# Moving a gate behind a decoding operation, splitting two gated blocks early, and emptying an accumulator before the next gate

## The chip, the cores and the metric

The kernel runs on one core of a Trainium2 chip. Its engines are TensorE (PE in the rows; its weight loads are PEld), VectorE (DVE), ScalarE (ACT), GpSimd (POOL) and SyncE (SP), which issues nearly all loads. Each engine works through its own list of instructions in order and waits on semaphores for the others. The metric is the device time of one execution in microseconds (us).

## The reference, cut to what matters

Three layers follow each other: a windowed attention, a gated feed-forward layer, and a layer of 8 experts with a router. The change lies in the second:

```python
def _moe_ref(x, w_in, w_out):
    h = x @ w_in                        # 3072 x 512 by 512 x 2048
    relu6 = np.clip(h + 3.0, 0.0, 6.0)
    g = h * relu6 / 6.0                 # the gate
    return (g @ w_out).astype(np.float32)
```

The weights `w_in` and `w_out` come as 64-bit floats and are taken as pairs of 32-bit integers.

## The kernel before, in words

The 3072 tokens go through the feed-forward layer in blocks. Block 0 holds four tiles of 128 tokens (512 columns), block 1 two tiles, each later block three. The 2048 hidden features are cut into 16 groups of 128; a pass is the work on one group `f`. Each product is made exact enough by three matmuls, because every operand is kept as a rounded high half and the low rest: high by high, low by high and high by low.

Block 0 is special, since the weights are decoded while it runs.

**First stage** (`mm1(0, f)`, matmuls at L395). In pass `f` TensorE multiplies group `f + 1` (12 matmuls of 512 columns into one of two banks, `h0` and `h1`), then `dec(1, lambda: gate0(f, hp))` decodes one piece of weights and gates group `f`. `decode_w` takes piece `n` from a raw tile (three buffers) with three VectorE operations: the first (L369) writes `d`, the second (L372) adds bits to `d`, the third (L373) writes the float in `dec` (two buffers). Then `load_w(n + 3)` asks SyncE for the next raw tile, ScalarE rounds the piece to its high half (L378), and GpSimd subtracts for the low half (L379). In pass `f` piece `n = f + 3` is decoded, so from pass 13 on the pieces are those of `w_out` (n = 16 and above). The gate is an activation on ScalarE (L431) and a multiplication on VectorE (L433); it frees the bank that TensorE wants for group `f + 2`. The gated block is put somewhere until the second stage (`g_home`): for the last two groups that is a `dec` buffer. Attention steps of tiles 4 to 6 stand between the passes (`side`): `a` (transposes of queries and keys, copies into `kt`), `s` (scores, maximum, exponential), `n` (sums), `p` and `v` (probabilities times values, after which SyncE issues 16 small loads), `x` (result transposed and split).

**Second stage** (`mm2(0, f)`, matmuls at L451). The groups come in the order `STEP` = 14, 15, 0, 1, ... 13. For each, `split_g` rounds the gated block into its high half on ScalarE (L439) and subtracts for the low half (L440; GpSimd, for one group VectorE), and TensorE adds 12 matmuls of 512 columns into four accumulators: three banks `acc`, and the bank `h0`. Meanwhile pieces 18 to 31 are decoded with `d` in the bank `h1`.

**Block 1 and later.** `mm1(1, 0)` (12 matmuls of 256 columns into `h1`), its gate (L408, L409) and its split (L403, L404) are followed by `evac(0)`, which empties the four accumulators of block 0, two on VectorE (L468) and two on ScalarE (L470). `mm1(1, 1)` writes to `h0`, the fourth accumulator's bank.

Of the kernel before, what the change touches and what calls it, by code (L numbers as in the profile page):

```python
# [7 lines left out]
F32 = mybir.dt.float32  # L8
# [6 lines left out]
ALU = mybir.AluOpType  # L15
# [15 lines left out]
def attn_moe_kernel(ctx, tc, q, k, v, mem_k, mem_v, w_in, w_out, emb, tau, w1, w2, out, dbg=None):  # L31
# [322 lines left out]
    def decode_w(n, first=None):  # L354

        f = FORD[n]
        t = raw.pop(n)
        if n < KF:
            t = t.rearrange("p c n t -> p (c n) t")
            dst_h, dst_l = w_in_h[:, :, f * P:(f + 1) * P], w_in_l[:, :, f * P:(f + 1) * P]  # L360
        else:
            for hl in range(2):
                if (hl, f // 2) not in wo:
                    wo[hl, f // 2] = pair(hl, f // 2, F32R)
            dst_h, dst_l = (wo[hl, f // 2][:, f % 2, :] for hl in range(2))
        lo, hi = t[:, :, 0], t[:, :, 1]
        d = late["dw"]().bitcast(I32)
        w = sb.tile([P, 512], I32, tag="dec", name="dec", bufs=2)
        nc.vector.tensor_scalar(out=d, in0=hi, scalar1=0x07FFFFFF, scalar2=3, op0=ALU.bitwise_and, op1=ALU.logical_shift_left)  # L369
        if first:  # L370
            first()
        nc.vector.scalar_tensor_tensor(out=d, in0=lo, scalar=29, in1=d, op0=ALU.logical_shift_right, op1=ALU.bitwise_or)  # L372
        nc.vector.scalar_tensor_tensor(out=w, in0=hi, scalar=-0x40000000, in1=d, op0=ALU.bitwise_and, op1=ALU.bitwise_or)  # L373
        load_w(n + 3)
        wf = w.bitcast(F32)
        if n < KF:
            wf = wf.rearrange("p (c n) -> p c n", c=KD)
        nc.scalar.copy(out=dst_h, in_=wf)  # L378
        nc.gpsimd.tensor_tensor(out=dst_l, in0=wf, in1=dst_h.bitcast(F32), op=ALU.subtract)  # L379
# [33 lines left out]
    def g_home(f):  # L413

        n_ = BS[0] * P
        if f >= KF - 2:
            return [(sb.tile([P, n_], F32, tag="dec", name="g0", bufs=2), 0, n_)]
        if f >= KF - 4:
            if f == KF - 4:
                keep["r"] = sb.tile([P, BT], F32, tag="g", name="g0r", bufs=1)  # L420
            w = "gh" if f == KF - 4 else "gl"
            o = (f % 2) * P
            return [(sb.tile([P, BT], F32, tag=w, name="g0", bufs=2), 0, BT), (keep["r"][:, o:o + P], BT, n_)]
        if f % 2 == 0:
            keep["p"] = pair(1, f // 2 + 1, F32)
        return [(keep["p"][:, f % 2, :], 0, n_)]

    def gate0(f, hp):
        keep[f] = g_home(f)
        for g, a, z in keep[f]:  # L430
            nc.scalar.activation(out=g, in_=hp[:, a:z], func=AF.Relu, bias=three)  # L431
        for g, a, z in keep[f]:
            nc.vector.scalar_tensor_tensor(out=g, in0=g, scalar=6.0, in1=hp[:, a:z], op0=ALU.min, op1=ALU.mult)  # L433

    def split_g(t, eng=None):
        f = STEP[t]
        gh, gl = (xT[0][i][1][:, 1 + t % 2, :] for i in range(2))
        for g, a, z in keep.pop(f):
            nc.scalar.copy(out=gh[:, a:z], in_=g)  # L439
            (eng or nc.gpsimd).tensor_tensor(out=gl[:, a:z], in0=g, in1=gh[:, a:z].bitcast(F32), op=ALU.subtract)  # L440
        g_t[0, f] = (gh, gl)
# [301 lines left out]
    def T_x(n, px=None):  # L743
        xg = xg_t.pop(n)
        gate = small([P, 1], name="m_gate", bufs=4)
        V.tensor_copy(out=gate, in_=xg[:, DM:DM + 1])
        m_t[n] = (gate, m_t[n])
        px = bank("att", 1) if px is None else px
        for j in range(KD):
            nc.tensor.transpose(px[:, j * P:(j + 1) * P], xg[:, j * P:(j + 1) * P], ident)  # L750
        th = sb.tile([P, KD + KE, P], F32R, tag="xh", name="th", bufs=2)
        tl = sb.tile([P, KD + KE, P], F32R, tag="xl", name="tl", bufs=2)
        x3 = px.rearrange("p (j s) -> p j s", j=KD)
        nc.scalar.copy(out=th[:, 0:KD, :], in_=x3)  # L754
        V.tensor_tensor(out=tl[:, 0:KD, :], in0=x3, in1=th[:, 0:KD, :].bitcast(F32), op=ALU.subtract)  # L755
        xt_t[n] = (th, tl)
# [168 lines left out]
    with tc.manual_schedule():  # L925
# [119 lines left out]
        for f in range(KF):  # L1045
            nxt = mm1(0, f + 1) if f + 1 < KF else None
            if f < KF - 1:
                dec(1, lambda: gate0(f, hp))
            else:
                gate0(f, hp)  # L1050
            if f in side:
                side[f]()
            hp = nxt
        a4[5]()
        split_g(0)
        split_g(1, nc.vector)
        pdw2 = bank("h", 2)
        late["dw"] = lambda: pdw2
        side = {0: a5[0], 2: a5[1], 3: a5[2], 4: a5[3], 6: a5[4], 8: a5[5], 9: a6[0], 10: a6[1], 12: a6[2], 13: a6[3], 15: a6[4]}
        for t in range(KF):  # L1060
            mm2(0, STEP[t], first=STEP[0], last=STEP[-1])
            if t + 2 < KF:
# [12 lines left out]
        for bl in range(NB):  # L1075
            slot, pre_ = {}, {}
            if bl == 0:
                continue
            if bl + 1 < NB:
                if bl == 1:  # L1080
                    slot[0] = [a6[5]]
                for a in range(bl == 1, TB):
                    st = stages(F0[bl + 1] + a)
                    for o, f_ in zip((0, 2, 3, 4, 6, 7) if bl == 1 else (0, 1, 2, 3, 4, 5), st):
                        slot.setdefault((1, 8)[a - 1] + o if bl == 1 else 5 * a + o, []).insert(0, f_)
            if bl:
                d = 2 if bl == 1 else 0
                for t in range(BS[bl - 1]):
                    (wt, f), (wl, f2) = (RT4 if bl == 1 else RT)[t], (RL4 if bl == 1 else RL)[t]
                    (pre_, slot)[wt].setdefault(f, []).append(lambda t=t: r_t(bl - 1, t, spare(bl)))  # L1090
                    (pre_, slot)[wl].setdefault(f2, []).insert(0, lambda t=t: r_l(bl - 1, t))
                    slot.setdefault((8, 8, 9, 9)[t] + d // 2, []).append(lambda t=t: r_ss(bl - 1, t))
                slot.setdefault(8 + d, []).append(lambda: r_route(bl - 1))
                slot.setdefault(9 + d, []).append(lambda: r_rank(bl - 1))
                slot.setdefault(10 + d, []).append(lambda: r_sel(bl - 1))
                slot.setdefault(11 + d, []).append(lambda: r_list(bl - 1))
                slot.setdefault(12 + d, []).append(lambda: r_exp(bl - 1))
                slot.setdefault(12 + d, []).append(lambda: r_gate(bl - 1))
                if bl == EB + 1:
                    slot.setdefault(12, []).append(pick_first)  # L1100
                    slot.setdefault(14, []).append(pick_rest)
            if bl == NB - 1:
                at_ctx.close()
                p2["pool"] = ctx.enter_context(tc.tile_pool(name="p2", bufs=1, side="right", reuse_waits="tile"))
                for n in range(NE):
                    load_x(("E", n))
                eE = [nc.values_load(e0i[0:1, n:n + 1], engines=[SP], min_val=0, max_val=E - 1) for n in range(2)]
                todo = [(st, p, i) for p in range(4) for st in range(2) for i in range(2)]
                rws = {}

                def pre(n=1):
                    for _ in range(n):
                        if todo:
                            st, p, i = todo.pop(0)
                            rws[st, p, i] = load_half(p, i, eE[st])

                def go(st, p, i, eng=None):
                    split_half(st, p, i, rws.pop((st, p, i)), eng)
                    pre()

                pre(RW)
                for n, f in enumerate(SP_):
                    slot.setdefault(f, []).append(lambda n=n: go(n // 2 % 2, n // 4, n % 2, nc.gpsimd if n in PG else None))
                slot.setdefault(1, []).append(plan_const)
                slot.setdefault(13, []).append(lambda: T_x(("E", 0)))
            mm1(bl, 0)
            if bl:
                evac(bl - 1)
            for f in range(KF):
                for g_ in pre_.get(f, []):  # L1130
                    g_()
                if f + 1 < KF:
                    mm1(bl, f + 1)
                for g_ in slot.get(f, []):
                    g_()
                if bl < NB - 1 or f < KF - 1:
                    mm2(bl, f)
# [147 lines left out]
```

## Time and profile before

| | us |
|---|---|
| median of 3 runs | 1066.66 |
| lowest and highest run | 1066.11, 1069.86 |
| the profiled execution | 1062.98 |
| its span | 1061.2 |

The span is what the profile shows from first to last instruction; the profiled execution took 1.8 us more. Its mean granted TensorE clock is 0.985 of full speed.

### The profile page before, as it was taken

How to read it: one execution, taken by the hardware profiler on the slowest of the kernel's cores; microseconds unless marked ns; L12 is line 12 of the kernel's file. 1: busy time of each engine (PE TensorE's matmuls, PEld its weight loads, DVE VectorE, ACT ScalarE, POOL GpSimd, SP SyncE). 2: the span in 40 equal slices, each digit the busy share in tenths (PEclk: the TensorE clock that was granted, in tenths of full speed). 3: DMA queues.
4: the chain of work that ended last, by engine and by line, in shares of the span. 5: the costliest groups of instructions: out<-in, count | busy, mean ns of one | idle time of the engine just before them, and what ended most of it. 6: DMA issues, size and time to landing. Idle time of an engine off the chain costs nothing.

```text
span 1061.2 us, 22705 instructions
## 1 busy us (share of the span) xinstructions
PE 1013.5 (96%) x8350; PEld 855.5 (81%) x8350; DVE 519.3 (49%) x1194; ACT 429.4 (40%) x769; POOL 153.4 (14%) x155
## 2 busy tenths in 40 slices
PE   8787998999999999999999999998999999999994
PEld 4565777878888888888888888886888888888883
DVE  5676774554544544544544454755124433326530
ACT  5343443434333433434424424562235434336531
POOL 1133670000000000000000000043112211112210
PEclk9899899999999999999999999998999999999998
DMA  9655441152121122122211023331134514347510
GB/s 193 147 157 173 144 140 39 39 71 44 40 60 39 39 61 45 30 61 48 46 52 38 11 70 107 125 98 64 38 111 152 167 52 134 103 138 245 207 50 22
DMA packets 133914, 95.50 MB, mean 90 GB/s; under 512 B 100789, under 2 KB 109013, under 8 KB 133792
## 3 DMA queue, kind: packets, MB, share of 16 engines
q1 hardware_dynamic: 129184, 80.51, 27.6%
q0 software_dynamic: 4448, 13.42, 3.9%
q8 instruction: 67, 1.10, 0.4%
q14 instruction: 55, 0.45, 0.1%
q10 hardware_dynamic: 160, 0.02, 0.0%
HBM read 156.83 MB, written 13.38 MB: 160 GB/s over the span
## 4 chain that ended last, share of the span: by engine, by line
PE 78%; DVE 7%; issue 5%; ACT 3%; DMA 2%; POOL 1%; SPq 1%; POOLq 0%; DVEq 0%; ACTq 0%
PE acc L451 22%; PE h L395 20%; PE acc L799 12%; PE h L768 12%; PE s L777 2%; PE s L182 2%; PE s L294 1%; PE s L236 1%; DVE dec L373 1%; PE att L750 1%; PE att L280 1%; PE att L182 1%; DMA out_dram<-r,m_tid 1%; DMA raw_in<-in_moe_w_in_dram 1%; PE att L488 1%
## 5 line engine op out<-in xcount | busy, mean ns | idle before, releaser
L451 PE MATMUL acc<-wo,gh 128*128 128x512 f32 x640 | 206.5, 404 | 0.5 <-DVE x L468 0.3
L395 PE MATMUL h<-xh,w_in_h 128*128 128x384 f32 (+2 forms) x512 | 176.2, 344 | 10.6 <-DVE wo L433 4.0
L395 PE MATMUL h<-xl,w_in_h 128*128 128x384 f32 (+2 forms) x512 | 173.1, 338 | 0.1
L395 PE MATMUL h<-xh,w_in_l 128*128 128x384 f32 (+2 forms) x512 | 172.6, 337 | 0.0
L408 ACT ACTIVATE g<-h,three 128x384 f32<-128x384 f32 (+1 forms) x112 | 63.4, 566 | 173.9 <-PE h L395 172.1
L409 DVE SCALAR_TENSOR_TENSOR g<-g,h 128x384 f32<-128x384 f32 (+1 forms) x112 | 59.7, 533 | 143.5 <-ACT g L408 143.4
L451 PEld LDWEIGHTS acc<-wo,gh 128*128 128x128 f32 x640 | 113.1, 188 | 20.0 <-DVE x L468 0.7
L451 PE MATMUL acc<-wo,gl 128*128 128x512 f32 x320 | 126.1, 394 | 0.0
L395 PEld LDWEIGHTS h<-xh,w_in_h 128*128 128x128 f32 x512 | 96.5, 188 | 21.1 <-DVE wo L433 6.9
L395 PEld LDWEIGHTS h<-xl,w_in_h 128*128 128x128 f32 x512 | 96.6, 189 | 7.1 <-DVE xl L331 1.0
L395 PEld LDWEIGHTS h<-xh,w_in_l 128*128 128x128 f32 x512 | 96.4, 188 | 2.9
L404 DVE TENSOR_TENSOR gl<-g,gh 128x384 fp32r<-128x384 f32 (+1 forms) x112 | 60.8, 543 | 63.2 <-ACT gh L403 63.2
L403 ACT CAST gh<-g 128x384 fp32r<-128x384 f32 (+1 forms) x112 | 55.8, 498 | 74.0 <-DVE g L409 74.0
L755 DVE TENSOR_TENSOR tl<-att,th 128x512 fp32r<-128x512 f32 x26 | 18.0, 691 | 114.7 <-ACT th L754 108.4
L538 POOL TENSOR_TENSOR rn_y<-ss,half 128x3 f32<-128x3 f32 (+2 forms) x8 | 6.9, 860 | 464.9 <-ACT junk L528 464.9
L451 PEld LDWEIGHTS acc<-wo,gl 128*128 128x128 f32 x320 | 60.1, 188 | 13.9 <-DVE gl L404 0.3
L736 POOL DMA_INDIRECT xg<-xb,m_ix x27 | 27.9, 1032 | 260.2 <-PE h L768 210.7
L799 PE MATMUL acc<-wo,th 128*128 128x512 f32 x192 | 60.6, 397 | 0.0
L754 ACT CAST th<-att 128x512 fp32r<-128x512 f32 x26 | 15.3, 587 | 106.6 <-PE acc L799 104.9
L771 ACT ACTIVATE hs<-h 128x512 f32<-128x512 f32 x54 | 32.1, 597 | 64.4 <-PE h L768 60.5
L799 PE MATMUL acc<-w_in_h,th 128*128 128x512 f32 x120 | 49.5, 412 | 0.0
L768 PE MATMUL h<-wo,th 128*128 128x512 f32 x192 | 48.9, 397 | 0.0
(311 smaller groups left out, 1845.9 us busy)
## 6 DMA issues: line engine op xcount, KB each, us to landing
rw<-in_moe_w_dram SPq DMA_DIRECT2D x136, 512.0 KB
vw<-in_v_dram SPq DMA_DIRECT2D x176, 56.0 KB
raw_in<-in_moe_w_in_dram SPq DMA_DIRECT2D x16, 512.0 KB
raw_out<-in_moe_w_out_dram SPq DMA_DIRECT2D x16, 512.0 KB
k_t<-in_k_dram SPq DMA_DIRECT2D x24, 256.0 KB
q_t<-in_q_dram SPq DMA_DIRECT2D x24, 256.0 KB
xb<-x SPq DMA_DIRECT2D x20, 256.5 KB
xb<-x SPq DMA_DIRECT2D x4, 256.0 KB
```

The costliest lines, as they stand in the source:

```text
L182: nc.tensor.transpose(dst[:, j * P:(j + 1) * P], t[:, 2 * j:2 * j + 2, :].rearrange("p a d -> p (a d)"), ident)
L395: nc.tensor.matmul(hp, lhsT=wt[:, c, f * P:(f + 1) * P], rhs=xc, start=(n == 0), stop=(n == 3 * KD - 1))
L403: nc.scalar.copy(out=gh, in_=g)
L404: nc.vector.tensor_tensor(out=gl, in0=g, in1=gh.bitcast(F32), op=ALU.subtract)
L408: nc.scalar.activation(out=g, in_=hp, func=AF.Relu, bias=three)
L409: nc.vector.scalar_tensor_tensor(out=g, in0=g, scalar=6.0, in1=hp, op0=ALU.min, op1=ALU.mult)
L451: nc.tensor.matmul(acc[bl][t], lhsT=gt[:, t * P:(t + 1) * P], rhs=wo[hl, f // 2][:, f % 2, :], start=(f == first and n == 0), stop=(f == l ...
L736: nc.gpsimd.indirect_dma_start(out=t[:, :], out_offset=None, in_=src, in_offset=bass.IndirectOffsetOnAxis(ap=ix[:, 0:1], axis=0), bounds_c ...
L768: nc.tensor.matmul(hp, lhsT=a[:, kk, :], rhs=wpart(st, hl, p, kk), start=(kk == 0 and a is th and hl == 0), stop=(kk == KD - 1 and a is tl))
L771: nc.scalar.activation(out=h_t[n][:, p, :], in_=hp_t.pop((n, p)), func=AF.Relu)
L777: nc.tensor.transpose(hp[:, j * P:(j + 1) * P], h[:, j * P:(j + 1) * P], ident)
L799: nc.tensor.matmul(o, lhsT=a[:, KD + f, :], rhs=wpart(st, hl, 2 + half, kk), start=(f == 0 and c == 0), stop=(f == KE - 1 and c == 2))
```

## The change

Three edits. In `decode_w` the gate (`first()`) now stands behind the second decoding operation and ahead of the third. The last two gated blocks of block 0 no longer go into `dec` buffers: 384 of their columns go into the second buffers of `gh` and `gl`, the other 128 into columns 256 to 383 of `g0r` (one place for both groups, used one after the other), and they are split on VectorE right behind their gate. The step `x` of tile 4 (`a4[5]`), which stood between the stages, now stands behind the second stage's first group, together with step `a` of tile 5. `evac(0)` now stands ahead of `mm1(1, 0)`.

```diff
@@ decode_w
         nc.vector.tensor_scalar(out=d, in0=hi, scalar1=0x07FFFFFF, scalar2=3, op0=ALU.bitwise_and, op1=ALU.logical_shift_left)
+        nc.vector.scalar_tensor_tensor(out=d, in0=lo, scalar=29, in1=d, op0=ALU.logical_shift_right, op1=ALU.bitwise_or)
         if first:
             first()
-        nc.vector.scalar_tensor_tensor(out=d, in0=lo, scalar=29, in1=d, op0=ALU.logical_shift_right, op1=ALU.bitwise_or)
         nc.vector.scalar_tensor_tensor(out=w, in0=hi, scalar=-0x40000000, in1=d, op0=ALU.bitwise_and, op1=ALU.bitwise_or)
@@ g_home
-        if f >= KF - 2:
-            return [(sb.tile([P, n_], F32, tag="dec", name="g0", bufs=2), 0, n_)]
         if f >= KF - 4:
             if f == KF - 4:
                 keep["r"] = sb.tile([P, BT], F32, tag="g", name="g0r", bufs=1)
-            w = "gh" if f == KF - 4 else "gl"
-            o = (f % 2) * P
+            w = "gh" if f % 2 == 0 else "gl"
+            o = min(f - KF + 4, 2) * P
@@ first stage and start of the second
                 gate0(f, hp)
+            if f in STEP[0:2]:
+                split_g(STEP.index(f), nc.vector)
             if f in side:
                 side[f]()
             hp = nxt
-        a4[5]()
-        split_g(0)
-        split_g(1, nc.vector)
         pdw2 = bank("h", 2)
         late["dw"] = lambda: pdw2
-        side = {0: a5[0], 2: a5[1], ...
+        x4, a50 = a4[5], a5[0]
+        side = {0: lambda: (x4(), a50()), 2: a5[1], ...
@@ blocks
+            if bl == 1:
+                evac(0)
             mm1(bl, 0)
-            if bl:
+            if bl > 1:
                 evac(bl - 1)
```

In the changed kernel the lines behind `g_home` have numbers that are 2 lower. On VectorE, in each of the first 15 passes of the first stage (here pass 0; `acc` is the bank that holds `d`, `wo` the home of the gated block):

```order
 L369 TENSOR_SCALAR acc<-raw_in 128x512
-L433 SCALAR_TENSOR_TENSOR wo_838<-wo_838,h_809 128x512
-L372 SCALAR_TENSOR_TENSOR acc<-raw_in,acc 128x512
+L370 SCALAR_TENSOR_TENSOR acc<-raw_in,acc 128x512
+L431 SCALAR_TENSOR_TENSOR wo_839<-wo_839,h_809 128x512
 L373 SCALAR_TENSOR_TENSOR dec<-raw_in,acc 128x512
```

The gate has changed places with the second decoding operation. On ScalarE, from the activation of group 14 on, before (`g_1314` and `g_1323` are groups 14 and 15):

```order
L431 ACTIVATE g_1314<-h_1269,three 128x512
L378 CAST wo_1282<-dec 128x512
L431 ACTIVATE g_1323<-h_1298,three 128x512
L329 CAST xh<-att 128x4x128
L439 CAST xh<-g_1314 128x512
L439 CAST xh<-g_1323 128x512
L439 CAST xh<-wo_838 128x512
L378 CAST wo_1358<-dec 128x512
```

And now (`g_1315` and `g_1329` with parts of `g0r`):

```order
L429 ACTIVATE g_1315<-h_1269,three 128x384
L429 ACTIVATE g0r<-h_1269,three 128x128
L378 CAST wo_1282<-dec 128x512
L437 CAST xh<-g_1315 128x384
L437 CAST xh<-g0r 128x128
L429 ACTIVATE g_1329<-h_1298,three 128x384
L429 ACTIVATE g0r<-h_1298,three 128x128
L437 CAST xh<-g_1329 128x384
L437 CAST xh<-g0r 128x128
L437 CAST xh<-wo_839 128x512
L378 CAST wo_1357<-dec 128x512
L329 CAST xh<-att 128x4x128
```

Group 14's two roundings stand ahead of group 15's activations, all four are in two parts, and the copy for step `x` of tile 4 (`xh<-att`) has moved behind the first rounding and the first decoding of the second stage. On VectorE at the start of block 1, before (`h_1930` is the product of `mm1(1, 0)`, `h_1343` the fourth accumulator):

```order
L301 TENSOR_TENSOR xo<-s_1887,sm 128x2x4x64
L409 SCALAR_TENSOR_TENSOR g<-g,h_1930 128x256
L404 TENSOR_TENSOR gl<-g,gh 128x256
L468 TENSOR_SCALAR x_1951<-h_1343 128x512
L468 TENSOR_SCALAR x_1950<-acc 128x512
```

And now:

```order
L301 TENSOR_TENSOR xo<-s_1895,sm 128x2x4x64
L466 TENSOR_SCALAR x_1939<-h_1342 128x512
L466 TENSOR_SCALAR x_1938<-acc 128x512
L409 SCALAR_TENSOR_TENSOR g<-g,h_1945 128x256
L404 TENSOR_TENSOR gl<-g,gh 128x256
```

Both accumulators of VectorE are emptied ahead of the gate and the split.

## Rows read from the trace of the kernel before

**Rows 1.** Page, part 1: busy time, share of the span, instructions

```profile
PE 1013.5 (96%) x8350; PEld 855.5 (81%) x8350; DVE 519.3 (49%) x1194; ACT 429.4 (40%) x769; POOL 153.4 (14%) x155
```

**Rows 2.** Stretches: length, busy time of each engine, clock, DMA share, GB/s

```profile
43.84:102.22 58.38, 52.19 (x332) 38.94 (x333) 40.60 (x70) 21.21 (x43) 18.59 (x15) 0.97 0.52 153
102.22:107.70 5.48, 0.60 (x6) 0.36 (x4) 2.63 (x5) 2.35 (x5) 1.66 (x2) 0.77 0.43 161
107.70:112.85 5.15, 5.01 (x13) 3.49 (x13) 3.61 (x5) 0.47 (x1) 1.28 (x1) 0.58 0.01 5
112.85:163.37 50.52, 49.18 (x465) 38.84 (x463) 34.27 (x60) 21.77 (x39) 36.82 (x33) 1.00 0.47 146
...
88.00:96.00 8.00, 6.02 (x25) 4.33 (x24) 5.22 (x10) 2.57 (x5) 2.58 (x2) 1.00 0.76 233
```

**Rows 3.** TensorE's waits, 40 to 170 us: total, times, longest

```profile
PE acc L451 <- ACT xh L439: 4.9, 1, 4.9
PE h L395 <- DVE wo L433: 4.0, 6, 1.6
PE h L395 <- DVE x L468: 2.6, 1, 2.6
PE h L395 <- DVE g0r L433: 2.2, 2, 1.7
```

**Rows 4.** Timeline of VectorE, one pass: start, length, [idle before, releaser]

```profile
86.92 0.69 DVE L433 SCALAR_TENSOR_TENSOR wo<-wo,h 128x512 f32<-128x512 f32 x1 [0.67 <-ACT wo L431]
87.52 0.69 DVE L372 SCALAR_TENSOR_TENSOR acc<-raw_in,acc 128x512 int32<-128x512 int32 x1
88.32 0.69 DVE L373 SCALAR_TENSOR_TENSOR dec<-raw_in,acc 128x512 int32<-128x512 int32 x1
...
90.28 0.69 DVE L433 SCALAR_TENSOR_TENSOR wo<-wo,h 128x512 f32<-128x512 f32 x1 [0.67 <-ACT wo L431]
```

**Rows 5.** Timeline of ScalarE in the same pass

```profile
89.04 0.62 ACT L378 CAST w_in_h<-dec 128x512 fp32r<-128x512 f32 x1 [2.15 <-DVE dec L373]
89.57 0.68 ACT L431 ACTIVATE wo<-h,three 128x512 f32<-128x512 f32 x1
```

**Rows 6.** Timeline of VectorE: gate of pass 2, behind the copies into kt

```profile
57.59 0.68 DVE L433 SCALAR_TENSOR_TENSOR wo<-wo,h 128x512 f32<-128x512 f32 x1
```

**Rows 7.** Chain that ended last, 79 to 96 us: start, length, what

```profile
82.31 4.11 DMA raw_in<-in_moe_w_in_dram
...
90.26 3.98 DMA raw_in<-in_moe_w_in_dram
```

**Rows 8.** Timeline of TensorE between the stages

```profile
99.33 0.47 PE L395 MATMUL h<-xh,w_in_h 128*128 128x512 f32 x1 [0.54 <-DVE g0r L433]
...
102.22 0.60 PE L182 MATMUL att<-ident,xo 128*128 128x128 f32 x4
107.70 1.22 PE L451 MATMUL acc<-wo,xh 128*128 128x512 f32 x2 [4.88 <-ACT xh L439]
```

**Rows 9.** Timeline of ScalarE: activation of group 15

```profile
105.97 0.69 ACT L431 ACTIVATE g<-h,three 128x512 f32<-128x512 f32 x1 [1.37 <-POOL wo L379]
```

**Rows 10.** Timeline of all engines: the low halves of groups 14 and 15

```profile
107.72 1.28 POOL L440 TENSOR_TENSOR xl<-g,xh 128x512 fp32r<-128x512 f32 x1 [1.79 <-ACT xh L439]
108.20 1.35 DVE L440 TENSOR_TENSOR xl<-g,xh 128x512 fp32r<-128x512 f32 x1 [0.22 <-ACT xh L439]
```

**Rows 11.** VectorE's groups by form: busy, mean ns, idle before

```profile
L404 DVE TENSOR_TENSOR gl<-g,gh 128x384 fp32r<-128x384 f32 x96 | 54.0, 563 | 55.7 <-ACT gh L403 55.7
```

**Rows 12.** Timeline of TensorE at the start of block 1

```profile
164.75 0.28 PE L395 MATMUL h<-xh,w_in_l 128*128 128x256 f32 x1
167.60 0.39 PE L395 MATMUL h<-xh,w_in_h 128*128 128x256 f32 x1 [2.58 <-DVE x L468]
```

**Rows 13.** Timeline of VectorE there

```profile
163.58 0.69 DVE L301 TENSOR_TENSOR xo<-s,sm 128x512 f32<-128x512 f32 x1 [6.35 <-PE s L294]
...
166.87 0.68 DVE L468 TENSOR_SCALAR x<-h 128x512 f32<-128x512 f32 x1
```

More of the change, by code (lines that the diff above doesn't have):

```diff
@@ L1053, in attn_moe_kernel @@
             hp = nxt
-        a4[5]()
-        split_g(0)
-        split_g(1, nc.vector)
         pdw2 = bank("h", 2)
         late["dw"] = lambda: pdw2
-        side = {0: a5[0], 2: a5[1], 3: a5[2], 4: a5[3], 6: a5[4], 8: a5[5], 9: a6[0], 10: a6[1], 12: a6[2], 13: a6[3], 15: a6[4]}
+        x4, a50 = a4[5], a5[0]
+        side = {0: lambda: (x4(), a50()), 2: a5[1], 3: a5[2], 4: a5[3], 6: a5[4], 8: a5[5], 9: a6[0], 10: a6[1], 12: a6[2], 13: a6[3], 15: a6[4]}
         for t in range(KF):
```

## The prediction, as it was put on record before the changed kernel ran

> **What bounds the kernel now.** I began with the page's busy shares: TensorE is busy 96% of the span [rows 1], so time can only be won where TensorE stands still or runs slowly. The stretches show where that is near the edits. In the first stage (43.84 to 102.22) it is busy 52.19 of 58.38 us. Between the stages (102.22 to 107.70) it does 0.60 us of work, and the 12 matmuls that follow take 5.15 us at a mean clock of 0.58. In the second stage (112.85 to 163.37) only 1.3 of 50.5 us are idle [rows 2]. The waits name the causes: 6.2 us in eight waits for the gate on VectorE (L433), 4.9 us in one wait for ScalarE's rounding between the stages (L439), 2.6 us in one wait for `evac` on VectorE (L468) [rows 3]. Each edit aims at one of these. The 13.7 us, and some 2.4 us of slow clock behind the long one, are all there is to win.
>
> **Edit 1, the gate behind the second operation.** One pass without attention work is a closed loop [rows 4, 5]: gate to second operation 0.60, to third 0.80, to ScalarE's rounding 0.72, to the next activation (behind the rounding in ScalarE's list) 0.53, to the next gate 0.71. The sum, 3.36, is the distance between two gates (86.92 to 90.28). VectorE stands idle for 0.67 us ahead of the gate, with the first operation already done. With the second operation there as well, the loop is 0.60 + 0.72 + 0.53 + 0.71 = 2.56. VectorE's own four operations need 0.60 three times and, the second now right behind the first, 0.60 to 0.80 once (I take 0.7): 2.5. TensorE's 12 matmuls need up to 2.9 (99.33 to 102.22 [rows 8]; a little less without a wait ahead of them). So TensorE becomes the slowest, and a pass can win about 0.5.
>
> Passes with attention work win less. I walked all 15 with these durations. In pass 2 the copies into `kt` already make VectorE the late one: its gate has no idle time ahead of it [rows 6]. Now two operations stand ahead of it, and it comes 0.35 later than before. The gates' gain over the old starts runs: pass 1 0.55, pass 2 -0.35, passes 3 and 4 0.45, pass 5 0.55 (sums on VectorE), then 1.35, 2.1 and 2.9 in passes 6 to 8. The third operation of pass 8, no longer behind the second, gains 3.7. From there loads rule. That operation releases the raw tile whose load begins at 82.31 and takes 4.11 us. The 16 small loads of step `v` hold SyncE until 90.26, when the next raw load goes out and takes 3.98 [rows 7]. These 11.9 us don't shrink, while passes 9 to 11 do: VectorE's wait for that tile grows from 1.9 to about 2.7 us (estimates of my walk), and the gate of pass 12 stands behind one more operation. The gain of 3.7 is kept, and no more is added: the last group's product begins at 95.65 in place of 99.33 [rows 8] and ends at 98.45. **Gain 3.7**; bounds 0 (attention work or loads hold every pass) and 6.2 (every wait of rows 3 for the gate).
>
> **Edit 2, the last two blocks.** Before: the activation of group 15 waited until GpSimd had read a `dec` buffer (1.37 of idle [rows 9]); ScalarE's roundings stood behind it and behind step `x`; TensorE waited 4.88 [rows 8] and then ran slowly [rows 2]. From the end of the last product to the end of group 14's matmuls: 112.85 - 102.22 = 10.63.
>
> After, in my walk: the third operation of pass 14 at 98.15, ScalarE's rounding of piece 17 0.72 later, then the 384 columns of group 14, done at 99.95. TensorE begins there, 1.5 us after its last product. Its third matmul needs the low half. That subtraction on VectorE has two inputs in SBUF, and GpSimd works on piece 17's low half from 99.55 to 100.85. Before, just this pair met: VectorE's took 1.35 us for 512 columns and ended 0.55 after GpSimd's (109.55 against 109.00) [rows 10], where 384 columns cost 0.563 elsewhere [rows 11]. I take it as held until GpSimd is done: 101.3. Group 15's second activation needs the shared columns of `g0r` free, and so waits for the 128-column rest of that subtraction (101.6); gate 15 ends at 102.75. The fourth accumulator, in the bank which that gate frees, is wanted at 102.9: just in time. Ten matmuls at full clock (0.23 apart) from 101.3 end at 103.8 with the handovers: 5.35 in place of 10.63, less 0.43 for the four transposes of step `x`, which now follow. **Gain 4.85.** Bounds: 5.75 if GpSimd doesn't hold the subtraction; 2.4 if the clock still falls. I take the full clock: 1.7 us of idle at 94 to 96 left it at 1.00 [rows 2].
>
> The Trainium skill (SBUF — State Buffer, "Who interferes with whom") says that such a subtraction and a GpSimd operation that reads SBUF share a read interface, that whoever starts first holds it for the whole instruction, and that this is no halving of speed. The trace's one meeting agrees, by where VectorE's ended. By halved speed the low half would be ready 0.35 earlier, and the total gain that much larger.
>
> **Given back in the second stage.** Step `x`'s rounding and subtraction, done between the stages before, now stand among the first decodings. Piece 18: third operation at 105.3. ScalarE then has four items in a row (rounding 0.72, step `x` 0.50, two copies 0.95); VectorE's copies into `kt` end at 108.7, the three operations for piece 19 at 111, its rounding at 111.7, GpSimd's low half (1.28 [rows 10]) at 113.0. TensorE wants it at 111.6. Before, all waits of this stage together were 1.3 [rows 2]. **Loss 1.4 to 1.5**; bounds 0 and 4.85 (all that edit 2 won). Later pieces keep the old rhythm.
>
> **Edit 3, `evac` first.** `mm1(1, 0)` ends at 164.87 and `mm1(1, 1)` waits until 167.60 for L468, which stood behind the gate and the split [rows 12, 13]. Now VectorE empties the bank right behind step `v` (163.58 + 0.60): from 164.2 to 164.9. TensorE loses 0.1 in place of 2.7. The gate began at 165.63 when ScalarE was done with `mm1(1, 0)`'s result, and VectorE is free by 165.4, so it isn't late. ScalarE's two accumulators (L470) take 1.1 us while it would be idle. **Gain 2.65**; bounds 0 and 2.7.
>
> **The sum.** 3.7 + 4.85 - 1.5 + 2.65 = 9.7. The profiled execution would go from 1062.98 (span 1061.2) to 1053.3, the span to 1051.5. That execution is 3.7 below the median of the runs (1066.66); the median would be 1057.0. After 170 us I expect the old course, moved: TensorE paces it, and the loads are asked for by its progress.
>
> **The rivals.**
> 1. *Loads take edit 1's gain.* If the raw loads come later than the 4 us of rows 7 when asked for every 2.9 us, the first stage ends where it did: 9.7 - 3.7 = 6.0, time 1060.7. For it: the wait at pass 12, and a DMA share of 0.76 at 88 to 96 [rows 2]. Against: 0.52 over the stage, one such wait in 15 passes. Chance 0.12.
> 2. *The second stage takes edit 2's gain.* If decoding, once late, stays so, another 3.35 goes: gain 6.35, time 1060.3. For it: GpSimd is busy 36.8 of 50.5 us there, in pairs of 1.28 per group. Against: that leaves it 0.8 per group to catch up. Chance 0.10.
> 3. *The slow clock stays between the stages.* 12 matmuls took 5.15 where 2.75 is due: 2.4 less gain, 7.3, time 1059.4. Against: an idle time of 1.5, not 4.88. Chance 0.06.
> 4. *Slower: the gate is late in every pass.* If VectorE, not ScalarE, comes last everywhere, as in pass 2, each gate comes 0.7 later and TensorE waits for it: 13 times 0.7 is 9.1 lost in place of 3.7 won, 9.7 - 12.8 = -3.1, time 1069.8. It decides from 0.45 per pass on, where it eats the other edits' 6.0. Against: the 0.67 of idle ahead of the gate, released by ScalarE, in the plain passes [rows 4]. Chance 0.03.
> 5. *`evac` changes nothing*, a new wait in front of `mm1(1, 1)`: 7.05, time 1059.6. Chance 0.02.
>
> **How the numbers follow.** My forecast, gains of 8 to 12 us, has 0.67: its own range is 1054.7 to 1058.7. The gains with all bounds good (6.2 + 5.75 + 2.7, nothing given back) end at 1052; the first two rivals at 1060.7. The runs before spread over 3.8 us. The range is 1053.3 to 1060.9. What a measurement can tell from no change is about 0.5%, 5.3 us. Rivals 1 and 2 with some noise can fall within it, so faster has 0.90, no change 0.07, slower 0.03.
>
> **What would show it.** Right: gates in passes 9 to 11 about 2.8 apart, TensorE's waits for the gate (L431 in the changed kernel) short but for pass 12; group 14's first matmul about 1.5 us behind the last product at full clock, its third held by a subtraction that ends after GpSimd's; a wait for piece 19's low half of 1 to 2 us; no wait ahead of `mm1(1, 1)`. Wrong: raw tiles awaited in most passes; waits for GpSimd of over 3 us in the second stage; a clock of 0.5 between the stages.

## The result, and the profile after

The changed kernel took 1054.58 us (median of four runs, 1052.54 to 1056.5), the kernel before 1066.38 in the same comparison (1064.23 to 1069.86): a ratio of 0.9886, interval 0.9853 to 0.9919, or 12.2 us less, between 8.6 and 15.7. Forecast were 1057.0 and faster. The profiled execution took 1054.06 with a span of 1052.4; the one of before had 1062.98 and 1061.2.

The page's busy times after. TensorE does the same work [rows 1] in 8.8 us less:

```profile
PE 1013.7 (96%) x8350; PEld 857.0 (81%) x8350; DVE 520.4 (49%) x1199; ACT 431.2 (41%) x773; POOL 152.5 (14%) x154
```

TensorE's waits from 40 to 170 us after (total, times, longest). Those for the gate went from eight to four, the one for ScalarE's rounding from 4.9 to 1.3, the one for `evac` is gone [rows 3]:

```profile
PE h L395 <- DVE wo L431: 2.3, 3, 1.0
PE h L395 <- DVE g0r L431: 1.6, 1, 1.6
PE acc L449 <- ACT xh L437: 1.3, 1, 1.3
...
PE acc L449 <- POOL wo L379: 0.8, 2, 0.6
...
PE acc L449 <- DVE xl L438: 0.6, 1, 0.6
```

**First stage.** VectorE's timeline after, passes 10 to 12 (start, length, [idle before, releaser]). Gates are 2.56 apart (84.80, 87.36), with no idle time ahead of them, where they were 3.36 apart with 0.67 idle [rows 4]. Then VectorE stands still for 2.36 until a raw tile has landed (the first operation of pass 12, at 91.00):

```profile
84.80 0.69 DVE L431 SCALAR_TENSOR_TENSOR wo<-wo,h 128x512 f32<-128x512 f32 x1
...
87.36 0.69 DVE L431 SCALAR_TENSOR_TENSOR wo<-wo,h 128x512 f32<-128x512 f32 x1
...
91.00 0.69 DVE L369 TENSOR_SCALAR acc<-raw_in 128x512 int32<-128x512 int32 x1 [2.36 <-DMA raw_in<-in_moe_w_in_dram]
92.33 0.55 DVE L431 SCALAR_TENSOR_TENSOR g<-g,h 128x384 f32<-128x384 f32 x1
```

The chain that ended last, after, goes through that load, and ahead of it through SyncE's queue, which issues the small loads of step `v` one by one (eight at L167 and eight at L157, from 80.13 to 86.76):

```profile
83.40 0.30 SPq L157
...
86.86 4.12 DMA raw_in<-in_moe_w_in_dram
```

**Between the stages.** TensorE's timeline after: the product ends at 99.06 (100.34 less 1.28 of idle), group 14's matmuls begin 1.28 later, and the third waits 0.63 for the low half on VectorE. The transposes of step `x` follow at 105.41, group 15 at 106.93:

```profile
100.34 0.73 PE L449 MATMUL acc<-wo,xh 128*128 128x512 f32 x2 [1.28 <-ACT xh L437]
101.70 0.50 PE L449 MATMUL acc<-wo,xl 128*128 128x512 f32 x1 [0.63 <-DVE xl L438]
...
105.41 0.89 PE L182 MATMUL att<-ident,xo 128*128 128x128 f32 x4
...
106.93 0.71 PE L449 MATMUL acc<-wo,xh 128*128 128x512 f32 x2
```

The stretches after (length; busy time and count of PE, PEld, DVE, ACT, POOL; clock, DMA share, GB/s) show the clock at half speed from 102.80 to 105.41, although TensorE had stood still for no more than 1.28 and 0.63 us:

```profile
98.90:102.80 3.90, 1.99 (x7) 1.22 (x7) 2.37 (x5) 2.08 (x5) 1.28 (x1) 0.97 0.39 151
102.80:105.41 2.61, 2.61 (x8) 1.90 (x6) 2.19 (x6) 0.90 (x3) 0.00 (x0) 0.50 0.00 0
105.41:156.52 51.11, 50.21 (x470) 39.76 (x469) 35.74 (x63) 23.25 (x42) 36.98 (x33) 0.99 0.48 145
```

**Block 1.** VectorE's timeline after: `evac` (L466) follows the last tile of attention `xo`, the gate is not late for it, and the second gate starts 1.92 us behind the first:

```profile
156.52 0.69 DVE L301 TENSOR_TENSOR xo<-s,sm 128x512 f32<-128x512 f32 x1 [6.35 <-PE s L294]
157.13 0.68 DVE L466 TENSOR_SCALAR x<-h 128x512 f32<-128x512 f32 x1
157.73 0.68 DVE L466 TENSOR_SCALAR x<-acc 128x512 f32<-128x512 f32 x1
158.56 0.42 DVE L409 SCALAR_TENSOR_TENSOR g<-g,h 128x256 f32<-128x256 f32 x1
...
160.48 0.42 DVE L409 SCALAR_TENSOR_TENSOR g<-g,h 128x256 f32<-128x256 f32 x1 [0.60 <-ACT g L408]
...
163.27 0.42 DVE L409 SCALAR_TENSOR_TENSOR g<-g,h 128x256 f32<-128x256 f32 x1 [0.72 <-ACT g L408]
```

**A ruler for all runs.** The first gate of block 0 starts between 46.9 and 51.7 us in the traces below, behind code that no kernel changes there. So I compare distances from it on, between four instructions of VectorE: the gates of passes 0 and 15, `xo` of tile 6, the third gate of block 1. Each number is the difference of two starts on VectorE's timeline, the last one that to the end of the span. The time is the median; the gain comes from the ratio to the kernel before, which ran beside each.

| kernel | gate 0 to 15 | to `xo` | to third gate | to the end | sum of first three | time | gain (interval) |
|---|---|---|---|---|---|---|---|
| before | 57.3 | 56.9 | 9.4 | 888.2 | 123.7 | 1066.4 | |
| changed | 52.8 | 54.2 | 6.7 | 889.1 | 113.8 | 1054.6 | 12.2 (8.6 to 15.7) |
| changed, again | 52.8 | 54.2 | 6.8 | 887.5 | 113.7 | 1053.6 | 11.6 (8.7 to 14.5) |
| edit 1 alone | 53.4 | 57.1 | 10.7 | 887.6 | 121.2 | 1060.0 | 4.9 (3.1 to 6.7) |
| edit 2 alone | 58.2 | 55.0 | 11.0 | 887.9 | 124.1 | 1062.6 | 3.3 (1.6 to 5.0) |
| edit 3 alone | 57.7 | 57.1 | 6.8 | 888.0 | 121.6 | 1061.0 | 4.3 (2.5 to 6.1) |
| edits 1 and 2 | 52.5 | 54.2 | 10.9 | 888.1 | 117.6 | 1057.3 | 8.7 (5.9 to 11.5) |
| these, `evac` wait filled | 52.7 | 54.2 | 9.5 | 886.5 | 116.3 | 1057.1 | 8.5 (6.3 to 10.8) |
| changed, gap filled | 52.5 | 54.0 | 6.7 | 887.0 | 113.3 | 1054.4 | 10.9 (8.2 to 13.5) |
| changed, piece 17 later | 51.5 | 54.1 | 6.7 | 888.7 | 112.4 | 1052.7 | 12.1 (9.2 to 15.1) |
| changed, small loads later | 50.9 | 54.1 | 6.8 | 887.3 | 111.7 | 1052.1 | 12.5 (9.5 to 15.4) |
| the last two together | 48.9 | 54.1 | 6.8 | 886.5 | 109.7 | 1049.6 | 16.3 (13.6 to 19.0) |
| these, piece 19 earlier | 49.0 | 54.3 | 6.7 | 887.5 | 110.1 | 1052.2 | 13.0 (10.6 to 15.6) |
| changed, piece 19 earlier | 53.2 | 54.1 | 6.7 | 887.0 | 114.1 | 1053.7 | 12.2 (9.8 to 14.4) |

By the ruler the change won 9.9 us up to the third gate; what comes behind keeps its length within some 2.7 us from trace to trace. In 12 of the 13 rows below the first the gain in the time is larger than the gain by the ruler, by 1.7 us on the average of all 13, and in kernels with and without edit 3 alike. All of them are held against one trace of the kernel before, so that trace may be shorter than most of its executions.

### The profile page after: what moved, and what is told of

Same layout as the page of the kernel before. It is cut to its first block, busy times and chain, and to the rows that moved or that the text cites. A ratio compares the mean times of both kernels' runs of the same rounds, so it can differ in the third digit from the quotient of the medians.

```text
span 1052.4 us, 22716 instructions
## 1 busy us (share of the span) xinstructions
PE 1013.7 (96%) x8350; PEld 857.0 (81%) x8350; DVE 520.4 (49%) x1199; ACT 431.2 (41%) x773; POOL 152.5 (14%) x154
## 4 chain that ended last, share of the span: by engine, by line
PE 79%; DVE 6%; issue 6%; DMA 3%; ACT 2%; POOL 1%; SPq 1%; DVEq 0%; POOLq 0%; ACTq 0%
PE h L395 22%; PE acc L449 21%; PE acc L797 11%; PE h L766 11%; PE s L775 2%; PE s L182 2%; PE s L294 2%; PE s L236 1%; PE att L748 1%; PE att L182 1%; PE att L280 1%; DMA out_dram<-r,m_tid 1%; PE att L486 1%; DMA xg<-xb,m_ix 1%; DVE dec L373 1%
## 5 line engine op out<-in xcount | busy, mean ns | idle before, releaser
L449 PEld LDWEIGHTS acc<-wo,gh 128*128 128x128 f32 x640 | 113.2, 188 | 20.4 <-DVE x L466 1.0
```

The lines of the kernel that those rows point to most:

```text
L449: nc.tensor.matmul(acc[bl][t], lhsT=gt[:, t * P:(t + 1) * P], rhs=wo[hl, f // 2][:, f % 2, :], start=(f == first and n == 0), stop=(f == l ...
```

## The experiments

### The three edits apart

Edit 1 alone is the kernel before with this:

```diff
@@ decode_w
+        nc.vector.scalar_tensor_tensor(out=d, in0=lo, scalar=29, in1=d, op0=ALU.logical_shift_right, op1=ALU.bitwise_or)
         if first:
             first()
-        nc.vector.scalar_tensor_tensor(out=d, in0=lo, scalar=29, in1=d, op0=ALU.logical_shift_right, op1=ALU.bitwise_or)
```

> The kernel before with edit 1 alone (the gate behind the second decoding operation). Theory: the edits add up, and edit 1 is worth what the first stage lost between the two traces, 3.3 us (its last product ended at 98.9 in place of 102.2): time 0.3% lower; TensorE again waits about 4.9 us between the stages and 2.6 us for evac. Rival: its gain is lost again in the wait between the stages, which is set by ScalarE's list and not by TensorE: gain under 1 us.

Edit 2 alone takes the parts `g_home`, `split_g` and `side` of the diff above:

```diff
@@ first stage
+            if f in STEP[0:2]:
+                split_g(STEP.index(f), nc.vector)
...
-        a4[5]()
-        split_g(0)
-        split_g(1, nc.vector)
```

> The kernel before with edit 2 alone (last two gated blocks in free buffers and split at once, step x of tile 4 later). Theory of adding up: 3.8 us, the rest of the lead at the end of the second stage (7.1 - 3.3). Rival: without edit 1 the third operation of pass 14 comes later relative to TensorE, so TensorE still idles some 2.8 us between the stages, the clock falls there, and the gain is 2.5 us or less.

Edit 3 alone:

```diff
@@ blocks
+            if bl == 1:
+                evac(0)
             mm1(bl, 0)
-            if bl:
+            if bl > 1:
```

> The kernel before with edit 3 alone (accumulators of block 0 emptied ahead of the first gate of block 1). Theory: the wait of 2.6 us ahead of the second product of block 1 is gone and nothing replaces it: gain 2.3 to 2.7 us. Rival: a later wait takes it back within block 1 (the lead between the two traces fell from 9.3 us at 170 us to 8.8 us at the end): gain under 1.5 us.

And the changed kernel once more, beside the three:

> The changed kernel again, beside its parts on one chip. Theory: the profiled spans tell the size, 8.8 us, which is the sum of 3.3, 3.2 to 3.8 and 2.3. Rival: the medians of the timed runs do, 11.8 us, and the parts measured singly sum to that.

Measured: 1060.03, 1062.57, 1060.97 and 1053.6. In the time each edit wins, and the three gains (4.9, 3.3, 4.3) add up to 12.5, beside 11.6 for all of them; the intervals would allow some interplay. The traces do not add up: up to the third gate they have 2.5 us for edit 1, a loss of 0.5 for edit 2 and a gain of 2.1 for edit 3, beside 9.9 for all three. Edit 1 alone brings `xo` 3.8 us nearer to gate 0 (110.5 in place of 114.2), edit 2 alone only 1.1; on top of edit 1 it is 3.5. Alone, its gap between the stages was still 2.9 us long, and the clock fell: the signs of its rival. The time is 3.3 less, between the rival's 2.5 and the theory's 3.8, and the interval (1.6 to 5.0) holds both. Why the time shows a gain for edit 2 that its one trace does not show stays open.

Edit 1 alone did not do what was expected of it. The product ends only 1.4 us sooner behind gate 0 (100.87, 51.5 behind it, in place of 52.9): the wait at pass 12 is 2.1 there, and the clock is 0.50 at 96 to 98. The other 2.4 come from the wait between the stages, which was to stay at 4.9 and is 2.3. So edit 1 takes a part of what edit 2 was priced on. TensorE's waits in that trace:

```profile
PE acc L451 <- ACT xh L439: 2.3, 1, 2.3
PE h L395 <- DVE g0r L433: 2.1, 1, 2.1
```

Edit 3 alone shortens the way from `xo` to the third gate by 2.64 us, which is its wait; in the time it is 4.3, with an interval (2.5 to 6.1) that holds 2.64. The clock may make up the rest. In the trace of before the wait for `evac` is followed by a clock of 1.00, and the second gate of block 1 starts 4.2 us behind the first. In the trace of edit 1 alone the same wait is followed by half the clock. TensorE's wait there, and the stretch behind it:

```profile
163.87 0.58 PE L395 MATMUL h<-xh,w_in_h 128*128 128x256 f32 x1 [2.57 <-DVE x L468]
```

```profile
164.00:166.00 2.00, 2.00 (x10) 2.00 (x11) 0.41 (x1) 0.00 (x0) 0.00 (x0) 0.50 0.19 44
```

VectorE's timeline there: 5.4 us from the first gate to the second, which waits 2.93 us for ScalarE, that is for a product made at half clock:

```profile
161.90 0.42 DVE L409 SCALAR_TENSOR_TENSOR g<-g,h 128x256 f32<-128x256 f32 x1 [1.34 <-ACT g L408]
...
167.34 0.42 DVE L409 SCALAR_TENSOR_TENSOR g<-g,h 128x256 f32<-128x256 f32 x1 [2.93 <-ACT g L408]
```

### Edit 3 and the clock

The changed kernel without edit 3:

```diff
@@ blocks
-            if bl == 1:
-                evac(0)
             mm1(bl, 0)
-            if bl > 1:
+            if bl:
```

> Edits 1 and 2 without edit 3. Theory: the wait of 2.6 us ahead of the second product of block 1 is back and, as in the runs with edit 1 alone and edit 2 alone, is followed by some 2.5 us at a clock of 0.50: the two gates of block 1 that stand around it are 5.4 us apart, and the time is 3.9 to 4.2 us above the changed kernel. Rival: the clock holds at 1.00 as in the trace of the kernel before: 4.2 us apart, and 2.3 to 2.7 us above.

Measured: 1057.28, 8.7 us under before and 2.7 to 3.7 above the changed kernel's two medians, between the theory's figure and the rival's. In the trace the theory holds: the first two gates of block 1 are 5.4 apart, and the third stands 10.9 behind `xo`, as in the traces of edit 1 alone (10.7) and edit 2 alone (11.0). To see whether the clock makes the difference to the 9.4 of before, ten matmuls whose result nobody reads filled the wait:

```diff
@@ the same kernel
             mm1(bl, 0)
+            if bl == 1:
+                fill = bank("att", 1)
+                for _ in range(10):
+                    nc.tensor.matmul(fill, lhsT=w_in_h[:, 0, 0:P], rhs=w_in_h[:, 0, 0:512], start=True, stop=True)
```

> Edits 1 and 2 without edit 3, and ten matmuls of 512 columns whose result nobody reads, put on TensorE between the first product of block 1 and the emptying of the accumulators, in a free bank. In the traces with edit 1 or 2 but not edit 3 the 2.6 us wait is followed by a granted clock of 0.50, the third gate of block 1 starts 10.7 to 11.0 us after the last tile of attention (xo) on VectorE, and that tile is 898 to 899 us ahead of the end; the trace of before has the same wait at a clock of 1.00, 9.4 and 897.6. Theory (edit 3 is worth 2.65 for the wait and 1.4 for the clock behind it): TensorE is busy for 2.3 of the 2.6 us, the granted clock stays at 1.00, the third gate comes 9.3 to 9.6 behind xo although VectorE still empties the fourth accumulator ahead of the gate, and the kernel takes about 1.4 us less than edits 1 and 2 alone (1055.9 beside 1057.3). Rival (the longer distance of the gates comes from VectorE, which is late for the second gate as well): the clock is 1.00 and the third gate still comes 10.5 or more behind xo, 1057 or more.

In the stretch behind the wait, without and with the ten matmuls:

```profile
160.00:163.00 3.00, 2.91 (x13) 2.91 (x14) 0.63 (x2) 0.00 (x0) 0.00 (x0) 0.50 0.18 41
```

```profile
160.00:163.00 3.00, 2.89 (x21) 2.72 (x22) 1.07 (x3) 0.69 (x2) 0.00 (x0) 1.00 0.18 41
```

The clock stays at 1.00, and the third gate comes 9.46 behind `xo` with VectorE still late for the second: the theory's 9.3 to 9.6. So in the traces the clock is what the 1.4 us were lost to. That the ten matmuls kept it up is not shown: the kernel before kept it without them. The time, however, is 1057.11 beside 1057.28, where 1055.9 was expected. Intervals of two us to either side can't tell 1.4 from nothing, so in the time this effect is not shown.

### Between the stages: gap, clock, and what they are worth

Six matmuls whose result nobody reads, in a free bank, fill the 1.28 us:

```diff
@@ ahead of the second stage
+        fill = bank2()[:, 0, :]
+        for _ in range(6):
+            nc.tensor.matmul(fill, lhsT=w_in_h[:, 0, 0:P], rhs=xT[0][0][0][:, 0, :], start=True, stop=True)
```

> The changed kernel with six added matmuls of 512 columns (their result is not used) between the last product of the first stage and group 14's matmuls. Theory: the slow clock behind that place (0.50 for some 2.6 us, about 1.4 us lost) comes from the idle time of 1.3 and 0.6 us; with the first of these filled the clock stays at 1.00 and group 14's matmuls end about 1.4 us earlier. Of this up to 1.4 may go to a wait for piece 19's low half, which my prediction had and the changed kernel did not show. Rival: the clock falls for another reason (it falls in the stretch anyway): 0.50 again, and no gain.

TensorE's timeline in it. The 0.63 for the low half is still there; the clock held, and the transposes of step `x` begin 3.77 behind group 14's first matmul in place of 5.07. But a wait for GpSimd appears further on:

```profile
98.88 0.73 PE L449 MATMUL acc<-wo,xh 128*128 128x512 f32 x2
100.24 0.50 PE L449 MATMUL acc<-wo,xl 128*128 128x512 f32 x1 [0.63 <-DVE xl L438]
...
102.65 0.60 PE L182 MATMUL att<-ident,xo 128*128 128x128 f32 x4
...
111.83 0.50 PE L449 MATMUL acc<-wo,xh 128*128 128x512 f32 x1 [0.86 <-POOL wo L379]
```

The time is 1054.35, and `xo` stands 54.0 behind gate 15 in place of 54.2. Of the 1.3 us of clock that TensorE got back it then waits 0.86 for the low half of piece 19. Whether the six matmuls held the clock one trace can't tell: with piece 19 earlier (below) it held without them.

Next, ScalarE's rounding and GpSimd's low half of piece 17 go behind the split of group 14 (`late["tail"]` holds the two instructions until then), so that the split meets no work of GpSimd:

```diff
@@ decode_w
-        nc.scalar.copy(out=dst_h, in_=wf)
-        nc.gpsimd.tensor_tensor(out=dst_l, in0=wf, in1=dst_h.bitcast(F32), op=ALU.subtract)
+        def tail():
+            nc.scalar.copy(out=dst_h, in_=wf)
+            nc.gpsimd.tensor_tensor(out=dst_l, in0=wf, in1=dst_h.bitcast(F32), op=ALU.subtract)
+        if n == KF + 1:
+            late["tail"] = tail
+        else:
+            tail()
@@ first stage, behind split_g
+                if f == STEP[0]:
+                    late["tail"]()
```

> The changed kernel, with ScalarE's rounding of piece 17 and GpSimd's low half of it moved behind the split of group 14. Theory: VectorE's subtraction for group 14 takes 1.33 us only because GpSimd works at the same time; alone it takes 0.56 for its 384 columns. Group 14's matmuls then begin within 0.3 us of the last product, the third waits until about 1 us behind it, the clock stays at 1.00, and they end 3.3 us earlier; 0 to 1.5 of that is given back to a wait for the low half of piece 19. Gain against the changed kernel 1.8 to 3.3 us. Rival: the 1.33 us belong to the operation and its operands: it stays at 1.33, and the gain is 1.3 us or less.

VectorE's subtraction of group 14's 384 columns in the changed kernel, and the same in this one:

```profile
100.32 1.33 DVE L438 TENSOR_TENSOR xl<-g,xh 128x384 fp32r<-128x384 f32 x1 [1.10 <-ACT xh L437]
```

```profile
99.97 0.55 DVE L444 TENSOR_TENSOR xl<-g,xh 128x384 fp32r<-128x384 f32 x1
```

The subtraction takes 0.55, as the theory had it. No idle time is left between the stages, and the clock stays at 1.00. The gain of 1.8 to 3.3 did not come: the time is 1052.71, `xo` 54.1 behind gate 15, and the wait for piece 19 is there as well (0.86). What this kernel wins in the trace, 1.3 us, it wins ahead of gate 15 but for 0.1.

### The load of pass 12

The 16 small loads of step `v` of tile 4 are issued behind pass 12, not in it ahead of a raw load:

```diff
@@ step v of tile 4
-                    load_mv(i + 2)
-                    load_v(i + 2)
+                    if i == BS[0]:
+                        late["lv"] = lambda: (load_mv(i + 2), load_v(i + 2))
+                    else:
+                        load_mv(i + 2)
+                        load_v(i + 2)
@@ first stage
+            if f == 12:
+                late["lv"]()
```

> The changed kernel with the 16 small loads that step v of tile 4 asks for issued behind pass 12 instead of pass 8. Theory: they hold SyncE for some 8 us ahead of the raw load that pass 12 needs; without them VectorE's wait of 2.4 us there and TensorE's of 1.6 are gone, passes 9 to 13 keep 2.6 to 2.9 us each, and the first stage ends 1.6 to 2.4 us earlier. Rival: raw tiles are late by the rate of the loads; the wait moves to another pass and the stage ends within 0.5 us of where it did.

On VectorE's timeline the first operation of pass 12 follows the last of pass 11 (89.84, 0.68 long) without idle time:

```profile
89.84 0.68 DVE L373 SCALAR_TENSOR_TENSOR dec<-raw_in,acc 128x512 int32<-128x512 int32 x1
90.44 0.69 DVE L369 TENSOR_SCALAR acc<-raw_in 128x512 int32<-128x512 int32 x1
```

Gate 15 comes 1.9 us sooner behind gate 0, all of which reaches the third gate (111.7 in place of 113.7); time 1052.11. The loads did hold edit 1, by that much. The gap between the stages is shorter as well (0.85 and 0.64), the clock stays at 1.00 there, and the wait for piece 19 is 0.85.

### Both, and piece 19

The two edits above together:

> The changed kernel with two edits that have each run alone: ScalarE's rounding and GpSimd's low half of piece 17 behind the split of group 14, and the sixteen small loads of step v issued behind pass 12. Theory (TensorE has no idle time left between the stages, but from gate 15 on the second stage is held by the low half of piece 19, so that what is won between the stages is waited for there): granted clock 1.00 from 64 to 107 us, a wait of 0.9 us on GpSimd for wo in the third product of the second stage, 54.0 to 54.2 us from gate 15 to xo as in the changed kernel (54.2) and in both parts; about 1 to 1.5 us below the changed kernel, all of it from the wait of pass 12, 1051.5 to 1053. Rival (the stages' joint is what counts): xo 1.4 to 2 us closer to gate 15, and 1050 to 1051.5.

Measured: 1049.56, a ratio of 0.9847 (0.9822 to 0.9872): below the kernel before and, by 4.1 us, below the changed kernel with piece 19 earlier, which ran beside it and is its like in time. My theory had what follows gate 15 right (54.1, a wait of 0.86 for piece 19) and the total wrong, and so had the rival: neither expected gate 15 itself to come 3.9 us sooner. The two parts alone brought it 1.2 and 1.9. Most of the other 0.7 lies in pass 0: gates 0 and 1 are 3.06 and 3.11 apart in the traces of the parts, 2.80 in those of the changed kernel and of both together. Counted from gate 1, the parts bring 1.5 and 2.2, both together 3.9. TensorE's waits from 98 to 172 us in it:

```profile
PE acc L455 <- POOL wo L381: 1.7, 3, 0.9
```

From gate 15 to GpSimd's start on the low half of piece 19 it is 9.68 us here (95.82 to 105.50). It is 9.67 in the changed kernel (102.29 to 111.96), 9.69 with piece 17 later, 9.68 with the gap filled and 9.68 with the small loads later. GpSimd's rows in the changed kernel and in this one:

```profile
111.96 1.30 POOL L379 TENSOR_TENSOR wo<-dec,wo 128x512 fp32r<-128x512 f32 x1
```

```profile
105.50 1.28 POOL L381 TENSOR_TENSOR wo<-dec,wo 128x512 fp32r<-128x512 f32 x1 [1.63 <-ACT wo L380]
```

So what is won on TensorE alone between gate 15 and piece 19 is given back there, and what brings gate 15 forward counts in full. Two kernels decode piece 19 right behind piece 18, ahead of step `x` and the copies into `kt`; one on top of both edits, one on the changed kernel:

```diff
@@ second stage
-            dec()
+            for _ in range((2, 0)[t] if t < 2 else 1):
+                dec()
             if t in side:
```

> As the kernel before it in this list, and the decoding of piece 19 issued directly behind that of piece 18, ahead of the transposes and copies of K and Q that stood between. Theory (the low half of piece 19 holds the second stage once the joint is closed): VectorE begins piece 19 at once behind piece 18, 2.7 us earlier, the 0.9 us wait on GpSimd in the third product of the second stage goes, and xo comes 52.6 to 53.3 us behind gate 15 in place of 54.1; 0.8 to 1.5 us below the kernel without this edit. Rival (the copies of K and Q, now 2.2 us later on VectorE, hold the products of attention, so that the wait moves there): a wait for kt, qT or s of about 1 us takes its place and xo stays at 54.0 or later.

> The changed kernel with the decoding of piece 19 directly behind that of piece 18, and nothing else. Theory (the slow clock between the stages and the low half of piece 19 lie beside each other: TensorE comes to the third product of the second stage, in the changed kernel, no sooner than the low half is there): clock 0.50 between the stages as before, no wait for wo there with or without the edit, xo 54.0 to 54.3 us behind gate 15, time the same as the changed kernel's within 0.5 us. Rival (piece 19's place costs something of its own): xo 0.8 us or more closer to gate 15.

Measured: 1052.24 and 1053.67. The first is the rival's case, and its time is 2.7 above that of the kernel without this edit (0.3 by the ruler): TensorE's 0.86 for piece 19 is gone, but the copies into `kt` are late in its place, and `xo` stays 54.3 behind gate 15:

```profile
109.82 0.85 PE L236 MATMUL s<-kt,qT 64*32 64x64 f32 x64 [0.57 <-DVE kt L201]
```

The second takes the changed kernel's time, as expected, though not its clock: it stayed at 1.00 behind the same two idle times (1.29 and 0.62), where 0.50 was expected. So this run was no test of slow clock and early piece 19 together. It shows something else: TensorE had its 1.3 us of clock back and no wait for piece 19, and still `xo` came 54.1 behind gate 15. It waited 0.31 for `kt` and 0.35 for GpSimd on the way, and then, as in every kernel here that has edits 1 and 2, twice more for the low half of a later piece: 20.4 to 20.7 and 44.4 to 44.7 us behind gate 15. The second of these places in the changed kernel (gate 15 at 102.29) and in this one (102.55):

```profile
146.83 0.51 PE L449 MATMUL acc<-wo,xh 128*128 128x512 f32 x1 [0.63 <-POOL wo L379]
```

```profile
146.96 0.50 PE L449 MATMUL acc<-wo,xh 128*128 128x512 f32 x1 [0.67 <-POOL wo L379]
```

So it is not piece 19 alone that holds the second stage: the decoding of the pieces, counted from gate 15, reaches TensorE again later, whatever was won before.

## Why the prediction was right, step by step

The steps are read in the changed kernel against the kernel before, both counted from gate 0.

**Edit 1, 3.7.** The last product ends 3.3 sooner (49.6 in place of 52.9); with edit 1 alone it was 1.4. The 3.8 at `xo` and the 4.9 (3.1 to 6.7) of that kernel in the time are near the forecast by luck, since more than half of the 3.8 came from between the stages. The loop of 2.56 is what the gates show, and TensorE's waits for the gate are short but for pass 12. The sign "about 2.8 apart" did not come: TensorE's products begin 2.8 to 2.9 apart (80.10, 83.00, 85.88, 88.68), but it is ahead of the gates, and they catch up. The wait for the raw tile was put at 2.7 and is 2.36; from the third operation of pass 8 (its end, 78.98) to the landing of that tile (90.98) it is 12.0, where 11.9 were forecast not to shrink. Rival 4 (the gate late in every pass) fell with the 2.56. Rival 1 (loads take the gain) named a real wait and overrated it: without it another 1.9 can be had.

**Edit 2, 4.85 less 1.5.** The net of 3.35 is 3.9 in the changed kernel, but the way there was another. From the end of the product to the end of group 14's matmuls I had 5.35; it is 6.35 (99.06 to 105.41), so 3.85 were won there in place of 4.85. From there to `xo` nothing was given back, where I had 1.5. The idle times came out as the walk had them (1.28 where I had 1.5; the low half took 1.33 where I had 1.35). The step that failed is "I take the full clock": from 102.80 to 105.41 the clock is 0.50, which was rival 3 and one of the signs of being wrong. It cost 1.3 of TensorE's time, not that rival's 2.4. The row behind that step ends 0.2 us behind its idle time of 1.7; the clock did hold there, but with edit 1 alone an idle time of 2.1 at the same place was followed by 0.50. The low half of piece 19 was forecast to be done at 113.0 and is done at 113.26; I had TensorE wanting it 1.4 earlier, but TensorE, slowed by 1.3, came to it at 113.40 and did not wait. The slow clock and the loss at piece 19 lie beside each other, and only one of them counts; where the clock holds (gap filled), the wait shows (0.86) and `xo` is 54.0 behind gate 15 in place of 54.2. Rival 2 fell: all waits of that stage for GpSimd are 0.8.

**Edit 3, 2.65.** The distance from `xo` to the third gate fell from 9.43 to 6.75, by 2.68; rival 5 fell. Against kernels in whose trace the clock fell behind the wait it is 4.1 (10.88 less 6.75).

**The sum.** 9.7 were forecast, 9.9 are in the traces: 3.3, 3.85 and 2.7, with nothing given back. That the total is so near is in part luck: the first two terms came out 0.4 and 1.0 too large, the loss 1.5 too large. In the time it is 12.2 (8.6 to 15.7), and the median of the runs lies 2.4 below the forecast; the interval holds 9.7. The distance from `xo` to the third gate may be the difference: it is 9.4 in the one profiled execution of before and 10.7 to 11.0 in three other traces with the same wait. If the clock falls there in most executions of the kernel before, edit 3 is worth 4.1 and the sum 11.1 to 11.3. It would also fit the gains in the time that lie above the ruler's, but not the 3.3 of edit 2 alone. That is argued from traces of other kernels; no trace of another execution of before was taken for it, and filling the wait did not change the time by what could be measured.

## What to carry to other kernels

Before a wait is costed, look for the next instruction that depends on none of the work that the wait holds up: here the low halves of piece 19 and of later pieces, at fixed distances behind gate 15 (9.7 us to the first) whatever TensorE did in between. Gains ahead of gate 15 passed the second stage in full (two small moves brought gate 15 3.9 us nearer to gate 0 and the third gate of block 1 4.0), gains of TensorE alone behind it did not. Price each edit on the kernel with the others in it: edit 1 alone already halved the wait that edit 2 was priced on. And read the clock behind every idle time that an edit leaves, in more than one trace: it decided 1.3 us of TensorE's time here, and 1.4 at `evac`, though neither can be told from nothing in the kernel's time.

## What the runs showed of the hardware

The granted clock does not follow from the length of the last idle times in front of it. Between the stages idle times of 1.28 to 1.30 and 0.63 us were followed by 0.50 in four traces (the changed kernel twice, edits 1 and 2 without edit 3, and these with the `evac` wait filled), and 1.29 and 0.62 by 1.00 with piece 19 earlier. At `evac`, 2.58 was followed by 1.00 in the trace of before, and 2.57 or 2.58 by 0.50 with edit 1 alone, edit 2 alone, and edits 1 and 2.

VectorE's subtraction with two inputs in SBUF took 1.33 us for 384 columns when GpSimd had begun on its own 0.37 earlier (99.95, 1.28 long), and 0.55 without it. The Trainium skill (SBUF — State Buffer, "Who interferes with whom") has the one that issues first hold the shared read interface for its whole instruction. The trace agrees: VectorE's ended at 101.65, 0.42 behind GpSimd's, where 0.55 begun at GpSimd's end would give 101.78 and half speed beside GpSimd some 101.3 (estimates from these durations). The hold reached further than the 0.63 that TensorE waited: by the 128 columns behind it ScalarE's second activation of group 15 waited 0.92, and gate 15 another 0.43, and the second stage is counted from gate 15.
